# A fused attention and gated MLP kernel on one core: the written order of its operations is made anew from chunk 0's first product to chunk 7

## The chip, the core and the metric

The kernel runs on one core of a Trainium2 chip. That core has five engines with a queue each: TensorE (PE, with its weight loads shown as PEld), VectorE (DVE), ScalarE (ACT), GpSimd (POOL) and SyncE (SP). Each engine works through its own queue strictly in order, and waits at an instruction until the semaphores that it names have come. DMAs are issued from SyncE's, GpSimd's and ScalarE's queues. The metric is the device time of one execution in microseconds.

## What is computed

The reference is a linear attention followed by a two-layer MLP with a SiLU.

```python
# q, k, v: (8 batches, 8 heads, 576 positions, 64); w_in: 512x2048; w_out: 2048x512
q_s = softmax(q, axis=-1)                      # over the 64 of a head
k_s = softmax(k, axis=2)                       # over the 576 positions
kv  = einsum('bhsd,bhse->bhde', k_s, v)        # one 64x64 matrix per head
x   = einsum('bhsd,bhde->bhse', q_s, kv)       # then heads side by side: 4608 x 512
h   = x @ w_in
out = (h * sigmoid(h)) @ w_out                 # 4608 x 512
```

## The kernel before

The 4608 rows of x are cut into nine **chunks** (0 to 8) of 512 rows, while attention works by **batch** (0 to 7) of 576 rows. Chunk 0 is treated as wide: its first product takes all 576 rows of batch 0, and the 64 rows too many are handed to chunk 1 (`gcopy`).

Nearly all the work is written as small named operations, which the text ORDER (lines 18 to 66) lists in one sequence; line 807 calls them one after the other. There is no other scheduler: the place of a name in ORDER is its place in its engine's queue. Ahead of line 807 stands a prelude, written out as plain code (lines 545 to 621): the loads of batch 0 on SyncE, warm-up products (`heat`), batch 0's softmax and attention, the loads of w_in (W1) and of the first part of w_out (W2a) on POOL, and the first half of the contraction for the blocks 0 and 2 of chunk 0.

The names, with b a batch, t a chunk, and a number of a head pair, block or part behind them:

- `lq`, `lk`, `lv` load q, k, v (load, line 146). Batches 1 and 2 come through POOL's queue, later ones through SyncE's. `W2b1` to `W2d` load the rest of w_out (load_w2, line 569), `W1a0` to `W1d` stand for the parts of w_in (load_w1, line 563); both change the type on the way and go through POOL. Each name of batch b takes one of two buffers, so a load waits until the operation that reads the earlier contents is done.
- `eq`, `ek` are the exponentials (ACT, lines 163 and 168), `z` the sums of q (DVE, line 207), `n` the normalising (mostly POOL, line 216), `vc` the cast of v (POOL for batches 2 and later, line 144; ACT and DVE for batch 1). `qp1a` and `qp1b` are two adding steps of batch 1's sum on POOL (lines 181, 188). `tr1` and `tc1` transpose batch 1's q on TensorE and copy it out; `tq` does this by a DMA of SyncE for later batches.
- `kv` makes the head matrices (line 248), `kc` normalises and copies them (DVE, lines 259 and 261), `X`/`xt` make x transposed (line 282), and `x...a`/`x...v` copy it from PSUM on ACT or DVE (lines 142, 144).
- Chunk 0: `w` is a block of 128 columns of the first product (wide_mm, line 307), `h` its tanh (ACT, line 320), `v` the rest of the SiLU (DVE, line 323), `p0` to `p15` the second product (line 445), `po` its copy out (lines 458, 460), `os` its stores.
- Chunks 1 to 8: both products are done as 2x2 blocks in seven block products instead of eight, with sums of blocks made beforehand. `WS`, `xs`, `S`, `T` are those sums (DVE, lines 373, 383, 477, 487). `g t.g.i` is block product i of the first product (line 425, TensorE). Between them the running sum in PSUM is copied to a tile h (`s`, on ACT line 142 or DVE line 144), added again (`a`, DVE line 403), and passed through SiLU (`u`, ACT line 409). `b t.i.m` are the block products of the second product (line 503), `sa`, `sb`, `sc` snapshots (ACT, line 519), `wa`, `wb`, `wc`, `wl` the joining of results, `o` the stores. Half of chunk 1's first product is done plainly (`m`, line 335, SiLU `mu`, line 345).

A product that starts a new sum in a PSUM bank has to wait until the copy of the old sum has ended: so `g4.0.6` waits for `s4.0.0a`, `kv2` for `a1.1.1`, `m0` for `u1.1.4`.

The block that the change cuts in two is

```python
def wide_mm(fb, cs):
    for n in range(2):
        for c in cs:
            nc.tensor.matmul(out=PS[:, WIDE[fb] + n, 0:S // 2],
                lhsT=W1[:, c, fb * 128:(fb + 1) * 128],
                rhs=XTS[0][:, c, n * (S // 2):(n + 1) * (S // 2)],
                start=(c == 0), stop=(c == NC - 1))
```

with 16 blocks fb, and NC = 4 parts c of the contraction. W1a0 brings the parts 0 and 1 of blocks 0 to 3, W1a1 the parts 2 and 3.

Of the kernel before, what the change touches and what calls it, by code (L numbers as in the profile page):

```python
# [15 lines left out]


ORDER = """
    lk1.0 w1 lk1.1 w2 h1 w0 h2 v1 w3 h0 W2b1 w5 v0 v2 h3 w4 WS0.1 h5 w6 v3 h4 W2b2 v4 w7 v5 w8 h7 h6 v7 w9
    lv1.0 h8 v6 w11 v8 h9 lv1.1 w10 eq1.0.0 v9 h11 WS0.2 w12 eq1.1.0 v11 h10 w13 WS1.1 eq1.0.1 v10 h12 w15  # L20
    qp1a h13 v12 w14 eq1.1.1 v13 qp1b WS1.2 W2c1 p0 h14 z1.0 ek1.0 p1 z1.1.0 n1.0 z1.1.1 p2 h15 ek1.1 v15 p3
    WS1.4 W2c2 tr1.0 v14 lq2.0 p4 tc1.0a tc1.0b lq2.1 n1.1 p5 W2d p6 lk2.0 T1 vc1.0 lk2.1 p7 tr1.1 lv2.0
    vc1.1a vc1.1b gcopy WS1.3 kv1 lv2.1 tc1.1b p8 tc1.1a kc1 WS0.3 xt1.0 xt1.1 x1.0a x1.1v p9 x1.2a x1.3v
    g1.1.1 xs1.1 xs1.2 xs1.4 g1.1.2 s1.1.0a WS0.4 p10 xs1.3 eq2.0 a1.1.0 p11 eq2.1 z2.0 g1.1.6 g1.1.5
    s1.1.1a z2.1 n2.0 p12 ek2.0 g1.1.7 p13 s1.1.2v n2.1 ek2.1 p14 a1.1.2 g1.1.4 p15 tq2 u1.1.4 g1.1.3 po2v
    vc2.1 po1a m0 po3v po0a a1.1.1 u1.1.0 vc2.0 m1 lk3.0 mu0 m2 T2 lq3.0 mu1 lq3.1 m3 u1.1.2 lk3.1 T3 m4
    lv3.0 u1.1.1 lv3.1 m5 T4 mu2 os0 mu4 kv2 mu5 m6 mu3 kc2 X2.0 mu6 X2.1 x2.0v m7 x2.1a x2.3a x2.2v g2.1.1
    mu7 xs2.1 xs2.2 g2.1.2 s2.1.0v b1.1.0 ek3.0 S1.1 g2.1.6 eq3.1 lk4.0 S1.2 b1.2.0 os1 s2.1.1a b1.1.1 xs2.3
    xs2.4 eq3.0 a2.1.0 g2.1.7 vc3.0 sa1 b1.2.1 lq4.0 z3.1 s2.1.2a g2.1.5 vc3.1 ek3.1 b1.6.0 a2.1.2 n3.1
    lk4.1 g2.1.4 z3.0 g2.1.3 u2.1.0 g2.0.2 u2.1.4 wa1 n3.0 b1.6.1 a2.1.1 u2.1.2 g2.0.1 sb1 S1.3 kv3 tq3  # L30
    s2.0.0a b1.5.0 kc3 u2.1.1 S1.4 g2.0.6 b1.7.0 s2.0.1v lv4.0 ek4.1 b1.7.1 lv4.1 a2.0.0 os3 g2.0.7 sc1
    ek4.0 b1.5.1 s2.0.2v g2.0.5 eq4.0 lk5.0 wc1 lq4.1 g2.0.4 a2.0.2 os2 b1.4.0 vc4.0 lk5.1 z4.0 u2.0.4
    g2.0.3 u2.0.2 b1.3.0 lv5.0 vc4.1 a2.0.1 u2.0.0 lq5.0 b1.4.1 n4.0 X3.0 wl1v X3.1 kv4 x3.0a x3.1v x3.2a
    b1.3.1 kc4 x3.3a xs3.1 u2.0.1 g3.1.1 xs3.2 wb1 g3.1.2 s3.1.0a xs3.3 xs3.4 g3.0.2 S2.1 g3.1.6 S2.2 eq4.1
    b2.2.0 s3.1.1a b2.1.0 z4.1 ek5.0 b2.1.1 a3.1.0 g3.1.7 n4.1 sa2 ek5.1 b2.6.0 s3.1.2v g3.1.5 vc5.0 tq4
    g3.1.4 a3.1.2 u3.1.0 b2.6.1 u3.1.4 S2.3 g3.1.3 sb2 lq5.1 g3.0.1 u3.1.2 a3.1.1 lv5.1 lk6.0 b2.7.0 s3.0.0a
    o1.0 S2.4 b2.2.1 u3.1.1 a3.0.0 g3.0.6 lv6.0 b2.7.1 s3.0.1v eq5.0 g3.0.5 wa2 g3.0.7 sc2 lq6.0 z5.0 b2.4.0
    s3.0.2a lk6.1 b2.5.0 vc5.1 eq5.1 a3.0.2 g3.0.4 o1.1 n5.0 z5.1 g3.0.3 u3.0.4 b2.5.1 a3.0.1 n5.1 u3.0.0
    b2.4.1 wc2 u3.0.2 X4.0 X4.1 kv5 x4.1v x4.0a tq5 wl2v b2.3.0 u3.0.1 x4.3v g4.1.1 xs4.1 x4.2a b2.3.1 xs4.2
    s4.1.0a S3.1 g4.1.2 wb2 g4.1.6 lq6.1 a4.1.0 ek6.1 b3.1.0 xs4.3 s4.1.1a b3.1.1 xs4.4 S3.2 ek6.0 g4.1.5  # L40
    g4.1.7 sa3 eq6.0 b3.2.0 s4.1.2v eq6.1 b3.2.1 lq7.0 kc5 lk7.0 b3.6.0 a4.1.2 lv6.1 lq7.1 g4.1.4 o2.0 wa3
    g4.1.3 z6.0 u4.1.4 b3.5.0 u4.1.0 S3.3 g4.0.1 lk7.1 b3.6.1 a4.1.1 s4.0.0a g4.0.2 sb3 u4.1.1 g4.0.6 a4.0.0
    b3.5.1 s4.0.1a S3.4 b3.7.0 vc6.1 u4.1.2 g4.0.7 z6.1 vc6.0 g4.0.5 s4.0.2a b3.7.1 a4.0.2 n6.1 g4.0.4 sc3
    u4.0.2 g4.0.3 wc3 n6.0 b3.3.0 u4.0.4 a4.0.1 b3.4.0 u4.0.0 X5.0 X5.1 kv6 x5.0a x5.1v tq6 x5.3a x5.2v
    b3.3.1 u4.0.1 xs5.1 g5.1.1 xs5.2 wb3 b3.4.1 s5.1.0v o2.1 ek7.1 g5.1.2 kc6 g5.1.6 wl3a xs5.3 xs5.4 a5.1.0
    lv7.0 b4.2.0 s5.1.1a lv7.1 b4.1.0 S4.1 eq7.1 g5.1.7 ek7.0 b4.2.1 s5.1.2v o3.1 g5.1.5 S4.2 b4.1.1 u5.1.0
    a5.1.2 g5.1.4 sa4 g5.0.2 o3.0 u5.1.4 wa4 g5.1.3 S4.3 u5.1.2 vc7.1 g5.0.1 b4.6.0 a5.1.1 vc7.0 s5.0.0a
    b4.6.1 a5.0.0 u5.1.1 g5.0.6 S4.4 b4.5.0 s5.0.1a b4.5.1 sb4 u5.0.0 g5.0.7 g5.0.5 s5.0.2v b4.7.0 eq7.0
    a5.0.2 b4.7.1 z7.1 g5.0.4 sc4 g5.0.3 b4.4.0 a5.0.1 u5.0.4 b4.4.1 wc4 u5.0.1 X6.0 X6.1 kv7 x6.0v u5.0.2
    x6.3v b4.3.0 x6.1a kc7 b4.3.1 x6.2a xs6.1 xs6.2 g6.1.1 xs6.4 wl4v g6.1.2 S5.1 s6.1.0a b5.1.0 a6.1.0  # L50
    g6.1.6 xs6.3 g6.0.2 wb4 s6.1.1a S5.2 b5.1.1 o4.0 b5.2.0 S5.3 g6.1.7 S5.4 b5.2.1 s6.1.2a z7.0 g6.1.5 sa5
    g6.1.4 wa5 n7.0 b5.6.0 a6.1.2 u6.1.4 b5.6.1 g6.0.1 n7.1 sb5 u6.1.0 g6.1.3 s6.0.0a b5.7.0 a6.1.1 tq7
    b5.7.1 a6.0.0 u6.1.1 g6.0.6 sc5 b5.5.0 s6.0.1a o4.1 g6.0.5 u6.1.2 g6.0.7 b5.5.1 s6.0.2v b5.4.0 wc5
    g6.0.4 a6.0.2 b5.4.1 u6.0.4 b5.3.0 u6.0.2 X7.0 X7.1 x7.0a x7.1v g6.0.3 x7.2a xs7.1 u6.0.0 g7.1.1 x7.3v
    a6.0.1 b5.3.1 s7.1.0a xs7.2 g7.1.2 wl5a u6.0.1 g7.1.6 o5.1 a7.1.0 b6.1.0 s7.1.1a xs7.4 xs7.3 g7.1.5 wb5
    g7.1.7 S6.1 o5.0 b6.1.1 s7.1.2a S6.2 g7.0.2 sa6 a7.1.2 u7.1.0 g7.1.4 S6.3 b6.2.0 u7.1.4 g7.1.3 u7.1.2
    g7.0.1 a7.1.1 b6.2.1 s7.0.0a b6.6.0 wa6 u7.1.1 S6.4 g7.0.6 b6.6.1 s7.0.1v b6.5.0 sb6 a7.0.0 g7.0.7
    b6.7.0 s7.0.2a b6.7.1 b6.5.1 sc6 u7.0.0 g7.0.4 wc6 g7.0.5 u7.0.4 b6.4.0 a7.0.2 b6.3.0 X8.0 X8.1 x8.0v
    g7.0.3 x8.2a x8.1v u7.0.2 b6.4.1 xs8.1 a7.0.1 x8.3a g8.1.1 xs8.3 g8.1.2 s8.1.0a xs8.2 b6.3.1 wl6a u7.0.1
    g8.1.6 wb6 b7.1.0 S7.1 o6.0 s8.1.1a b7.2.0 a8.1.0 g8.1.7 o6.1 xs8.4 b7.1.1 S7.2 s8.1.2a g8.1.5 sa7  # L60
    u8.1.0 b7.2.1 a8.1.2 g8.1.4 S7.3 g8.1.3 u8.1.4 g8.0.2 a8.1.1 u8.1.2 g8.0.1 u8.1.1 b7.6.0 s8.0.0v b7.6.1
    wa7 g8.0.6 a8.0.0 sb7 b7.5.0 s8.0.1a S7.4 b7.7.0 g8.0.7 g8.0.5 s8.0.2v b7.7.1 a8.0.2 b7.5.1 sc7 u8.0.0
    g8.0.4 wc7 g8.0.3 u8.0.4 b7.4.0 a8.0.1 u8.0.2 b7.3.0 u8.0.1 b7.3.1 e1.0 wb7 S8.1b e1.1 o7.0 S8.1a b7.4.1
# [7 lines left out]
def kernel(  # L71
# [474 lines left out]
    nc.vector.memset(warm, 0.0)  # L546
# [2 lines left out]
    for name, src in (("qt", q), ("kt", k)):
        load(0, name, src, 0, nc.sync)  # L550
        if name == "qt":
            load(0, name, src, 1, nc.sync)
    load(0, "vt", v, 0, nc.sync)
    load(0, "kt", k, 1, nc.sync)
    load(0, "vt", v, 1, nc.sync)
# [19 lines left out]
    heat(20)  # L575
    exp_q(0, 0)
    qsum(0, 0)
    exp_q(0, 1)
    nc.gpsimd.tensor_copy(gate, st[0]["kt", 0][0:1, 1, 0:1])
    load_w1(0, 4, 0, 2)  # L580
    load_w1(0, 4, 2, 4)
    load_w1(4, 8)
    load_w1(8, 12)
    load_w1(12, 16)
    load(1, "qt", q, 0, nc.gpsimd)
    load(1, "qt", q, 1, nc.gpsimd)
    load_w2(0, 4)

    qnorm(0, 0, nc.vector)
    qsum(0, 1)  # L590
    exp_k(0, 0)
    tr(0, 0, 0, 5, 0)
    tr(0, 0, 5, J, 1)
    heat(7)
    qnorm(0, 1, nc.vector)
    vcast(0, 0, nc.scalar)
    trcopy(0, 0, 0, 5, 0, nc.scalar)
    trcopy(0, 0, 5, J, 1)
    kv(0, 0)
    kvcopy(0, 0, 1)  # L600
    tr(0, 1, 0, 5, 2)
    tr(0, 1, 5, J, 3)
    exp_k(0, 1)
    xt_mm(0, 0, 0, 320, 4, 0)
    xt_mm(0, 0, 320, 256, 0, 0)
    heat(3, 6)
    vcast(0, 1, nc.scalar, 0, 1)
    vcast(0, 1, nc.vector, 1, 2)
    trcopy(0, 1, 0, 5, 2, nc.scalar)
    trcopy(0, 1, 5, J, 3)  # L610
    kv(0, 1)
    kvcopy(0, 1, 2)
    heat(2, 3)
    xt_evac(0, 0, 4, 0, 320, 0, nc.scalar)
    xt_evac(0, 0, 0, 0, 256, 320, nc.vector)
    xt_mm(0, 1, 0, 320, 6, 0)
    xt_mm(0, 1, 320, 256, 2, 0)
    wide_mm(0, (0, 1))
    xt_evac(0, 1, 6, 0, 320, 0, nc.scalar)
    xt_evac(0, 1, 2, 0, 256, 320, nc.vector)  # L620
    wide_mm(2, (0, 1))
# [217 lines left out]
```

## Time and profile before

| what | value |
|---|---|
| median of 3 runs | 257.08 us (256.99 to 257.14) |
| profiled execution | 258.61 us, span of its instructions 256.6 us |
| TensorE busy | 249.1 us, 97% of the span |
| DVE, ACT, POOL busy | 206.2, 190.9, 65.8 us |
| DMA, mean over the span | 179 GB/s |
| chunk 0's first product begins | 14.96 us after the span's start |
| chunk 1's first `g2.1.1` | 61.69 us |
| last product ends | 248.6 us |

The profile is of one execution. Times in it count from the first instruction; "busy" is the time in which an engine works on an instruction, and the idle time before an instruction is put down to what ended it. Products overlap one another: a product of 256 columns takes 0.27 us from start to end, but the next starts 0.109 us later, so a group of eight takes 0.87 us from start to start. Times below that compare groups go from start to start.

### The profile page before, as it was taken

What the parts mean: (1) busy time and instruction counts of PE and PEld (TensorE: products, weight loads), DVE (VectorE), ACT (ScalarE), POOL (GpSimd) and SP (SyncE); (2) the same over time, 40 slices, a digit from 0 to 9 for tenths busy, and PEclk for the clock granted to TensorE, in tenths of its full rate; (3) what the DMA queues carried; (4) which work ended last, traced back from release to release, by engine and by line L of the source; (5) the groups of instructions that cost most, each with busy time, mean ns of one, the idle gap of its engine ahead of it and who ended that gap; (6) DMA issues with size and microseconds to landing.
All of it is one profiled execution on the core that took longest, in us unless ns stands there. A gap on an engine that the chain in (4) does not pass through costs nothing.

```text
span 256.6 us, 6459 instructions
## 1 busy us (share of the span) xinstructions
PE 249.1 (97%) x2732; PEld 204.2 (80%) x2732; DVE 206.2 (80%) x276; ACT 190.9 (74%) x225; POOL 65.8 (26%) x62
## 2 busy tenths in 40 slices
PE   8799999999999999999999999999999999999994
...
GB/s 248 348 181 297 302 301 283 351 140 393 378 128 213 403 187 137 361 335 168 276 266 68 224 236 3 3 52 32 163 14 153 13 0 4 148 18 0 66 141 123
DMA packets 36044, 45.89 MB, mean 179 GB/s; under 512 B 16288, under 2 KB 21088, under 8 KB 36016
## 3 DMA queue, kind: packets, MB, share of 16 engines
...
## 4 chain that ended last, share of the span: by engine, by line
PE 76%; DMA 11%; issue 5%; POOL 3%; ACT 2%; DVE 1%; ACTq 0%; POOLq 0%
PE PS L503 37%; PE PS L425 33%; DMA qt<-in_q_dram 5%; DMA kt<-in_k_dram 5%; PE PS L335 3%; PE PS L248 2%; PE PS L282 2%; POOL W L564 1%; DMA out_dram<-ow 1%; POOL qt L152 1%; DVE GT L323 1%; ACT L409 0%; POOL W L570 0%; ACT sg L320 0%; ACT GT L409 0%
## 5 line engine op out<-in xcount | busy, mean ns | idle before, releaser
L403 DVE TENSOR_TENSOR h<-PS,h 128x1024 f32<-128x1024 f32 (+1 forms) x45 | 54.2, 1206 | 9.3 <-PE PS L425 7.8
L503 PEld LDWEIGHTS <-GT 128*128 128x128 f16 x512 | 50.1, 98 | 5.9
L425 PEld LDWEIGHTS <-WS 128*128 128x128 f16 x480 | 46.7, 98 | 6.5 <-issue 0.6
L409 ACT ACTIVATE GT<-h 128x1024 f16<-128x1024 f32 (+1 forms) x45 | 46.8, 1051 | 0.9 <-DVE h L403 0.7
L503 PE MATMUL PS<-W,GT 128*128 128x256 f16 x384 | 47.3, 273 | 0.0
L425 PE MATMUL PS<-XS,WS 128*128 128x256 f16 (+1 forms) x360 | 45.0, 272 | 0.0
L142 ACT COPY h<-PS 128x1024 f32<-128x1024 f32 (+1 forms) x31 | 31.1, 1003 | 16.9 <-PE PS L425 15.7
L503 PEld LDWEIGHTS <-S 128*128 128x128 f16 x384 | 37.1, 98 | 4.6
L425 PEld LDWEIGHTS <-W 128*128 128x128 f16 x360 | 35.2, 98 | 4.4
L216 POOL TENSOR_TENSOR eq<-eq,rzq 128x1152 bf16<-128x1152 bf16 x13 | 27.3, 2115 | 37.6 <-DVE rzq L211 36.3
L503 PE MATMUL PS<-T,S 128*128 128x256 f16 x256 | 32.2, 273 | 0.0
L144 POOL CAST vaug<-vt 128x1152 bf16<-128x1152 f32 x12 | 15.8, 1328 | 61.5 <-DMA vt<-in_v_dram 61.4
L425 PE MATMUL PS<-XT,W 128*128 128x256 f16 (+1 forms) x240 | 29.7, 272 | 0.0
L144 DVE COPY h<-PS 128x1024 f32<-128x1024 f32 (+1 forms) x14 | 17.0, 1212 | 9.2 <-PE PS L425 4.4
L207 DVE TENSOR_REDUCE zq<-eq 128x18 f32<-128x1152 bf16 x14 | 18.8, 1342 | 4.1 <-ACT eq L163 4.0
L163 ACT ACTIVATE eq<-qt 128x1152 bf16<-128x1152 f32 (+1 forms) x18 | 18.9, 1055 | 3.1 <-DMA qt<-in_q_dram 2.8
L168 ACT ACTIVATE ek<-kt 128x1152 bf16<-128x1152 f32 x16 | 18.6, 1163 | 3.0 <-DMA kt<-in_k_dram 2.9
L791 POOL DMA_DIRECT2D out_dram<-ow x5 | 2.7, 545 | 70.0 <-DVE ow L773 70.0
L409 ACT ACTIVATE GT<-PS 128x1024 f16<-128x1024 f32 (+1 forms) x15 | 15.2, 1013 | 6.1 <-PE PS L425 6.1
L503 PE MATMUL PS<-T,GT 128*128 128x256 f16 x128 | 16.3, 272 | 0.0
L307 PE MATMUL PS<-XT,W 128*128 128x288 f16 x128 | 16.0, 286 | 0.2 <-DMA W<-in_moe_w_in_dram 0.2
L503 PE MATMUL PS<-W,S 128*128 128x256 f16 x128 | 16.1, 273 | 0.0
...
## 6 DMA issues: line engine op xcount, KB each, us to landing
...
```

The source lines that it names most:

```text
L142: eng.copy(out=o, in_=i)
L144: eng.tensor_copy(o, i)
L163: nc.scalar.activation(out=half(st[b]["eq"], cc)[:, :, g0:g1], in_=jgd(b, "qt", cc)[:, :, g0:g1], func=ACT.Exp)
L168: nc.scalar.activation(out=half(ek, cc), in_=jgd(b, "kt", cc), func=ACT.Exp)
L207: nc.vector.reduce_sum(out=z, in_=e, axis=AX.X)
L216: eng.tensor_tensor(out=e, in0=e, in1=r[:, :, :, None].to_broadcast([128, J, 2, D]), op=ALU.mult)
L307: nc.tensor.matmul(out=PS[:, WIDE[fb] + n, 0:S // 2], lhsT=W1[:, c, fb * 128:(fb + 1) * 128], rhs=XTS[0][:, c, n * (S // 2):(n + 1) * (S / ...
L335: nc.tensor.matmul(out=PS[:, bank, o0:TCH], lhsT=W1[:, c, fb * 128:(fb + 1) * 128], rhs=XTS[t % 2][:, c, o0:TCH], start=(c == 0), stop=(c ...
L403: nc.vector.tensor_tensor(out=four(t, i), in0=group_bank(t, g), in1=four(t, i), op=ALU.add)
L409: nc.scalar.activation(out=group_out(t, f, n), in_=x, func=ACT.Silu, scale=1.0 / XS)
L425: nc.tensor.matmul(out=PS[:, bank + p // 2, (p % 2) * HT:(p % 2) * HT + width(t)], lhsT=a[:, c, p * 128:(p + 1) * 128], rhs=bb[:, c, 0:wid ...
L503: nc.tensor.matmul(out=PS[:, bank, m * HN:(m + 1) * HN], lhsT=a[:, fc, m * 128:(m + 1) * 128], rhs=bb[:, fc, :], start=(first and fc == 0) ...
```

## The change

The prelude from the loads of batch 0 on becomes named operations too (`lq0.0`, `heat0`, `eq0.0`, `W1a0` and so on), with the same contents, and stands at the head of ORDER. Chunk 0's blocks become two operations each:

```diff
     for fb in range(NFB):
-        op(f"w{fb}", wide_mm, fb, range(2 if fb in (0, 2) else 0, NC))
+        op(f"w{fb}.0", wide_mm, fb, (0, 1))
+        op(f"w{fb}.1", wide_mm, fb, (2, 3))
```

ORDER is then written anew up to chunk 7; from `g8.1.4` on it is the old one. The prelude's operations keep their order on each engine, up to `x0.1`. SyncE's transfers keep theirs. Everything else is reordered, and no operation is added or dropped; the numbers of instructions on each engine stay. The places that matter below, old (-) and new (+), other names left out:

```diff
 first product, chunk 0
-    w1 w2 w0 w3 w5 w4 w6 w7 w8 w9 w11 w10 w12 w13 w15 w14 p0
+    w1.0 w1.1 w0.1 w2.1 w3.0 w3.1 w5.0 w4.0 w4.1 w5.1 w6.0 w7.0 w6.1 w7.1 w9.0 w8.0 w8.1 w9.1 w11.0 ... p0
 POOL, after W2a
-    lk1.0 lk1.1 W2b1 W2b2 lv1.0 lv1.1 qp1a qp1b W2c1 n1.0 W2c2 lq2.0 lq2.1 W2d lk2.0 lk2.1 lv2.0 lv2.1 n2.0 n2.1
+    W2b2 W2b1 lv1.0 lk1.1 qp1a lk1.0 lv1.1 qp1b W2c1 W2c2 n1.0 lq2.0 lq2.1 W2d lk2.0 lk2.1 lv2.0 n2.0 lv2.1 n2.1
 TensorE, chunk 1
-    p10 p11 g1.1.6 g1.1.5 p12 g1.1.7 p13 p14 g1.1.4 p15 g1.1.3 m0 m1 m2 m3 m4 m5 kv2 m6 X2.0 X2.1 m7 g2.1.1 g2.1.2
+    p10 g1.1.6 p11 p12 g1.1.7 g1.1.5 p13 g1.1.4 p14 g1.1.3 p15 m0 m1 m2 m4 m5 m3 kv2 m6 X2.0 X2.1 m7 g2.1.1 b1.1.0
 DVE, from a1.1.2 on
-    po2v po3v a1.1.1 T2 T3 T4 kc2 x2.0v x2.2v xs2.1 xs2.2 s2.1.0v S1.1 S1.2 xs2.3 xs2.4 a2.1.0 z3.1 a2.1.2 z3.0 wa1
-    a2.1.1 S1.3 kc3 S1.4 s2.0.1v a2.0.0 s2.0.2v wc1
+    T1 T2 T3 WS0.3 a1.1.1 WS0.4 po3v kc2 po2v x2.0v xs2.1 x2.2v xs2.2 s2.1.0v S1.1 xs2.4 xs2.3 a2.1.0 S1.2 z3.0 a2.1.2
+    z3.1 a2.1.1 wa1 S1.3 S1.4 a2.0.0 s2.0.1v T4 s2.0.2v kc3 wc1
 ACT, batch 1
-    h14 ek1.0 h15 ek1.1 tc1.0a vc1.0 vc1.1a gcopy tc1.1a x1.0a
+    h15 vc1.0 h14 ek1.1 ek1.0 tc1.0a vc1.1a tc1.1a gcopy x1.0a
 ACT, chunk 1
-    u1.1.4 po1a po0a u1.1.0 mu0 mu1 u1.1.2 u1.1.1 mu2 mu4 mu5 mu3 mu6 x2.1a
+    u1.1.4 po0a u1.1.2 mu0 mu1 u1.1.0 po1a mu2 mu5 mu4 u1.1.1 mu3 mu6 x2.1a
 TensorE, chunk 4
-    g4.0.1 b3.6.1 g4.0.2 g4.0.6
+    g4.0.1 X5.1 b3.5.1 g4.0.6
```

More of the change, by code (lines that the diff above doesn't have):

```diff
@@ L18 @@
 ORDER = """
[L19 to L63, printed above, removed]
@@ L64 @@
-    S8.2a sa8 S8.2b e2.0 wl7v e6.0 S8.3 o7.1 e6.1 e2.1 sb8 e5.0 waE0 S8.4 qa00g qa01s e7.0 waE1 e7.1 qa11g
-    qa10a e5.1 sc8 wcE0 e3.0 wcE1 qc01g wxE0 qc11a e3.1 wbE0 qc00a wxE1 qb00g qb01s e4.0 wbE1 qc10s qb10g
+    lq0.0 lq0.1 lk0.0 lv0.0 lk0.1 lv0.1 heat0 eq0.0 z0.0 eq0.1 gate W1a0 W1a1 W1b W1c W1d lq1.0 lq1.1 W2a n0.0 z0.1
+    ek0.0 tr0.0 heat1 n0.1 vc0.0 tc0.0a tc0.0b kv0.0 kc0.0 tr0.1 ek0.1 X0.0 heat2 vc0.1a vc0.1b tc0.1a tc0.1b kv0.1
+    kc0.1 heat3 x0.0a x0.0v X0.1 w0.0 x0.1v x0.1a w2.0 w1.0 w1.1 w0.1 h1 w2.1 v1 h0 w3.0 v0 h2 w3.1 w5.0 W2b2 w4.0
@@ new lines @@
+    h3 v2 w4.1 w5.1 v3 h4 w6.0 h5 v4 W2b1 w7.0 w6.1 v5 lv1.0 WS1.1 WS0.1 w7.1 h7 w9.0 w8.0 h6 v7 w8.1 v6 h8 w9.1 h9
+    lk1.1 eq1.0.1 eq1.0.0 w11.0 v8 w11.1 h11 v9 qp1a w10.0 lk1.0 w10.1 lv1.1 w12.0 h10 qp1b v11 w13.0 v10 eq1.1.1
+    w12.1 w13.1 w15.0 h12 h13 eq1.1.0 v12 W2c1 v13 w14.0 z1.0 w14.1 w15.1 p0 WS1.2 W2c2 h15 v15 z1.1.0 WS1.4 p1
+    vc1.0 n1.0 lq2.0 z1.1.1 h14 ek1.1 p2 p3 n1.1 ek1.0 p4 tr1.0 p5 tc1.0a v14 tc1.0b p6 tr1.1 WS1.3 vc1.1a tc1.1a p7
+    vc1.1b tc1.1b kv1 kc1 p8 xt1.0 xt1.1 gcopy WS0.2 x1.0a x1.2a x1.1v x1.3v lq2.1 p9 W2d lk2.0 xs1.1 xs1.2 lk2.1
```

117 lines of the change are left out of this document (64 added, 53 removed).

## Prediction

> **What bounds the kernel now.** I read the busy shares, the chain of work that ended last, TensorE's waits, and the timelines of the engines. The page gives
>
> ```profile
> PE 249.1 (97%) x2732; PEld 204.2 (80%) x2732; DVE 206.2 (80%) x276; ACT 190.9 (74%) x225; POOL 65.8 (26%) x62
> PE   8799999999999999999999999999999999999994
> PE 76%; DMA 11%; issue 5%; POOL 3%; ACT 2%; DVE 1%; ACTq 0%; POOLq 0%
> ```
>
> TensorE (PE) is the bound, and the order can only take away its waits. TensorE's waits, over the whole span, are few:
>
> ```profile
> PE PS L234 <- DVE eq L216: 1.3, 2, 0.9
> PE PS L561 <- DVE XS L546: 1.2, 1, 1.2
> PE PS L335 <- ACT GT L409: 0.6, 1, 0.6
> PE PS L445 <- DMA W<-in_moe_w_out_dram: 0.3, 1, 0.3
> PE PS L307 <- DMA W<-in_moe_w_in_dram: 0.2, 1, 0.2
> ```
>
> The first two lie before chunk 0's first product. All others end at 54.13 us; asked from 61 us to 250 us, the same view is empty. Products follow each other there at 0.87 us for 8, and that is the pace that the change can at best keep. So the prize is in the first 54 us, and the risk in everything after it.
>
> What ends those waits is seen in TensorE's timeline
>
> ```profile
> 16.55 14.63 PE L307 MATMUL PS<-XT,W 128*128 128x288 f16 x118 [0.19 <-DMA W<-in_moe_w_in_dram]
> ...
> 47.62 1.02 PE L445 MATMUL PS<-W,GT 128*128 128x512 f16 x4 [0.30 <-DMA W<-in_moe_w_out_dram]
> ```
>
> and in the chain, whose last DMA before 54 us is a load of k:
>
> ```profile
> 38.30 12.31 DMA kt<-in_k_dram
> ...
> 51.87 1.28 ACT L409
> 53.16 0.93 ACT GT L409
> ```
>
> Two landings gate the start: W2d at 47.6 us releases p12, and lk2.1 at 50.61 releases ek2.1, the table load and u1.1.4, which ends at 54.08 and releases m0 at 54.13. In windows from 8 to 51 us the DMA's busy share is 1.00 to 1.21 throughout, so both landings are set by bytes.
>
> **The change, part by part.** A time below is a start or duration of the profiled execution; two queued operations of DVE or ACT overlap by some 0.1 us, so I take start to start.
>
> 1. Halves of w1 and w0.1 ahead of w2.1. w1's third matmul needs W1a1, and the row above shows 0.19 us of idle there. In halves, four matmuls stand ahead of that need, not two: 2 x 0.12 = 0.25 us of cover. All of it (and 0.28 us that TensorE loses before tr1.0, by start to start) is worth nothing at the end if p12 still waits for W2d.
>
> 2. POOL's queue. W2b, lv1.0 and lk1.1 go first, lk1.0 and lv1.1 come behind qp1a, and lv2.1 behind n2.0. The transfers ahead of W2d and of lk2.1 are the same set as before, on one queue that stays filled (lk1.0's issue moves from 14.62 to about 28.3 us, behind qp1a's 1.28 us, while four transfers still wait), so I leave both landings where they are. lk1.0 then lands at about 36.5 us and not 31; ek1.0 follows, and kv1 still starts at about 39 us. TensorE reaches p12 at about 46.2 us, 1.4 us early. Gain at p12: none, the wait is only longer.
>
> 3. p12 to m0. One group, g1.1.5, moves behind p12. Before: 0.86 + 0.77 + 2x0.86 + 0.77 + 0.86 + 0.77 = 5.75 us from 47.62, and 0.76 us lost for u1.1.4. Now: 5.75 + 0.77 = 6.52 us, and m0 at 54.14. g1.1.5 fills what was a wait for u1.1.4, and the wait for W2d grows by as much. Net 0.0.
>
> 4. 54 to 62 us. T1, WS0.3, WS0.4 move here from 37 to 44 us, T4 leaves. On DVE from a1.1.2's end at 51.73: T1, T2, T3 at 1.14 each, WS0.3, WS0.4, po3v at 0.61 each, a1.1.1 at 1.0, 6.25 us, to 58.0; kc2 has to wait for kv2 until 59.75. The 1.8 us of cover holds the port waits below (at most 2 x 1.1). po2v comes before x2.0v: 60.45 + 0.6 = 61.0 against 60.89, and m7's end at 61.69 hides it. ACT does the same set from 53.16 in another order; mu6 waits for m6 as now. 0 to 0.4 us; I take 0.
>
> 5. DVE from 62 to 80 us. This is where I expect the loss.
>
> ```profile
> 62.95 1.22 DVE L144 COPY h<-PS 128x1024 f32<-128x1024 f32 x1
> ...
> 74.23 1.75 DVE L477 TENSOR_TENSOR GT<-GT 128x2048 f16<-128x2048 f16 x1
> 75.91 0.18 DVE L259 RECIPROCAL rz<-PS 128x4 f32<-128x4 f32 x1
> 76.12 0.49 DVE L261 TENSOR_TENSOR kvn<-PS,rz 128x128 bf16<-128x128 f32 x2
> 76.53 1.22 DVE L477 TENSOR_TENSOR S<-GT,S 128x2048 f16<-128x2048 f16 x1
> 77.69 1.22 DVE L144 COPY h<-PS 128x1024 f32<-128x1024 f32 x1
> 78.83 1.21 DVE L403 TENSOR_TENSOR h<-PS,h 128x1024 f32<-128x1024 f32 x1
> ```
>
> Without a gap worth naming, DVE works from s2.1.0v (62.95) to s2.0.1v (77.69), which ends at 78.91; g2.0.7 starts on TensorE at 79.16. The cover is 0.25 us. Now xs2.1 stands ahead of x2.2v and has to wait for x2.0v, so s2.1.0v starts about 0.25 us later. Behind it, up to s2.0.1v, kc3 leaves (76.53 - 75.91 = 0.62) and a2.0.0 comes in (1.14). s2.0.1v starts at 77.69 + 0.25 + 1.14 - 0.62 = 78.46 and ends at 79.68; g2.0.7 would be 0.52 us late. T4 comes right behind s2.0.1v, where DVE waited for g2.0.7 anyway, and costs nothing.
>
> 6. Collisions with POOL. T2 (1.65 us at 54.79) and T3 (2.17 us at 56.36) run beside POOL's two casts (54.20 to 57.46), T4 of the same shape takes 1.21 us at 58.45 with POOL idle; S1.3's 1.75 us beside n3.0 stands against 1.22 us for the other S. So a DVE operation with both inputs in SBUF can lose 0.4 to 1.0 us beside POOL. S1.2 moves from 65.34 to about 67.3 us, where POOL casts v of batch 3 (66.89, 2.63 us for two): 0 to 1.1 us, and S1.3 may lose its 0.53 us. I take +0.2 for both, by the S1.3 row. The Trainium skill, "SBUF — State Buffer", section "Who interferes with whom", says that a VectorE instruction with two SBUF inputs and a GpSimd instruction that reads SBUF exclude each other, whichever issued first holding the ports for its whole length. The trace agrees: T2 ends 1.2 us after the first cast's end, T3 1.1 us after the second's. By that rule S1.2 would wait for the rest of a cast, 0.7 us, and the sum would be 0.5 us higher.
>
> 7. Chunk 4's g4.0.1. It is followed by X5.1 and b3.5.1 alone before g4.0.6, which reuses the bank that s4.0.0a copies. Now that copy starts 0.25 us after the product's end (126.82 against 126.57) and takes 1.01; with 0.04 for the return 1.30 us. X5.1 is half of a 0.46 us pair, b3.5.1 0.87: 1.10 us of cover. Late by 0.2 us; before, b3.6.1 and g4.0.2 (1.74 us) hid it.
>
> 8. Chunks 5 to 7. Counted in the same way, every other such return that the old order does not have too keeps 0.04 us of cover or more: 0, with 0.2 us as the upper end for many thin covers. SyncE's order is the same.
>
> Sum: 0 + 0 + 0 + 0.52 + 0.2 + 0.2 = 0.92 us. The profiled execution has 256.6 us of span in 258.61 us; it becomes about 259.5. The median of the three runs stands 1.53 us below that execution, at 257.08; so I forecast **258.0 us**, 0.4% slower. Ends: without 5's late arrival and the collisions +0.2; with S1.2 at its worst (0.9 more), 4's 0.4 and 8's 0.2, +2.2.
>
> **Rivals.**
>
> *No change within 0.2%* (256.57 to 257.59; about what a measurement of this kernel can tell from no change). s2.0.1v comes in time, because S1.3 no longer meets n3.0 (-0.53) and S1.2 meets no cast. Then only the bank of g4.0.6 is left: 257.08 + 0.2 = 257.3 us. For it: the casts come when v has landed, and tq2 goes out about 1 us earlier. Against: DVE's 0.25 us of cover. Chance 0.26.
>
> *Faster: the landings come earlier.* W2d and lk2.1 are slowed in a patch: from 42 to 44 us the DMA moves 173 and 205 GB/s, from 45 to 49 us 379 to 408. If a new order of the queue takes that patch away, W2d lands up to 1 us earlier, u1.1.4 with it, and TensorE, which now has work in front of m0, uses it: 257.08 - 1.2 + 0.4 = 256.3 us. Against: same bytes, same queue, same neighbours of W2d. That the halves and the shorter waits ahead of p12 alone gain (0.25 + 0.28) needs the same early landing. Chance 0.14.
>
> *Slower by more: k of batch 1 late.* POOL holds lk1.0 until qp1a has run, and ACT does ek1.1, ek1.0, tc1.0a, vc1.1a in one row behind it. If lk1.0 lands after 37.9 us (36.5 by my count, plus the 1.4 us of cover at p12), each further us shifts p12, and with it the end. At 39 us: 258.0 + 1.1 = 259.1 us. Chance 0.10.
>
> That the change doesn't do what it says can be left out: SyncE's rows are the same, and the other queues carry the new order.
>
> **How the numbers follow.** Forecast (258.0) 0.50, no change (257.3) 0.26, early landings (256.3) 0.14, late k (259.1) 0.10. The range of 8 in 10 leaves out half of the early landings and half of the late k: 256.6 to 259.1. Faster by over 0.2%: 0.14. Slower by over 0.2%: the forecast and late k, 0.60. Within: 0.26.
>
> **What would show it.** Step 2 and 3: TensorE's row of p12 starts at 47.6 with about 1.4 us of wait, m0 at 54.1 with none. Step 5: a new wait of g2.0.7 (L425) for DVE's h (L144) of about 0.5 us near 79.5 us. Step 6: S1.2 longer than 1.22 us. Step 7: a wait of L425 for ACT's h (L142) of 0.2 us near 130 us. I am wrong if p12 starts before 47 us, if TensorE has no wait from 61 us on, or if waits show in chunks 5 to 7.

## The result, and the profile after

The changed kernel takes 260.14 us (median of 4 runs, 259.74 to 261.45) against 257.11 us (4 runs, 256.99 to 257.73) measured beside it: a ratio of 1.0122, 95% interval 1.0081 to 1.0162. Measured again (e9 below) the ratio was 1.0113 (1.0095 to 1.0130). So the changed kernel is 3.0 us slower; 0.92 us slower was forecast. The profiled execution took 259.84 us, with a span of 257.9 us.

On its page TensorE is still the bound; it works 1.2 us longer than before, and DVE 3.1 us longer, though neither has an instruction more:

```profile
PE 250.3 (97%) x2732; PEld 204.6 (79%) x2732; DVE 209.3 (81%) x276; ACT 190.5 (74%) x225; POOL 65.9 (26%) x62
...
PE 73%; DVE 11%; DMA 6%; ACT 5%; issue 1%; SPq 1%; POOL 1%; ACTq 0%; POOLq 0%; DVEq 0%
```

TensorE's waits (engine, line, what it waited for: us in total, times, the longest) have changed their releasers. The waits for W2d, W1a1 and the SiLU of L409 are gone, and waits for DVE's copies and additions of h and for a SiLU of DVE (L323) have come. The second to fourth line lie ahead of chunk 0's first product:

```profile
PE PS L425 <- DVE h L144: 1.3, 2, 1.0
PE PS L554 <- DVE XS L546: 1.2, 1, 1.2
PE PS L248 <- ACT vaug L142: 0.7, 2, 0.5
PE PS L234 <- DVE eq L216: 0.2, 1, 0.2
PE PS L248 <- DVE h L403: 0.2, 1, 0.2
PE PS L234 <- DVE GT L323: 0.2, 1, 0.2
```

In TensorE's timeline (start, us, what) chunk 0's first product has no wait, p12 (46.47, within a row of L445) has none, and the waits of L425 and L248 stand at g1.1.4 (50.86) and kv2 (59.05):

```profile
15.31 15.85 PE L307 MATMUL PS<-XT,W 128*128 128x288 f16 x128
...
50.86 0.93 PE L425 MATMUL PS<-XS,W 128*128 128x224 f16 x8 [0.96 <-DVE h L144]
...
54.11 4.70 PE L335 MATMUL PS<-XT,W 128*128 128x448 f16 x24
59.05 0.82 PE L248 MATMUL PS<-vaug,ek 64*64 64x65 bf16 x72 [0.23 <-DVE h L403]
```

DVE's timeline has no gap above 0.11 us from 45.5 to 59.5 us, and three operations with both inputs in SBUF are slow, xs1.4 (46.61), T2 (53.24) and T3 (55.23). The reduction z2.1 (48.22) takes its usual 1.34 us, though POOL rests at that time:

```profile
46.61 1.68 DVE L383 TENSOR_TENSOR XS<-XT,XS 128x448 f16<-128x448 f16 x1
48.22 1.34 DVE L207 TENSOR_REDUCE zq<-eq 128x18 f32<-128x1152 bf16 x1
...
49.77 1.03 DVE L144 COPY h<-PS 128x896 f32<-128x896 f32 x1
...
51.92 1.29 DVE L487 TENSOR_TENSOR T<-W 128x2048 f16<-128x2048 f16 x1
53.24 2.06 DVE L487 TENSOR_TENSOR T<-W,T 128x2048 f16<-128x2048 f16 x1
55.23 2.17 DVE L487 TENSOR_TENSOR W<-W 128x2048 f16<-128x2048 f16 x1
...
57.92 1.07 DVE L403 TENSOR_TENSOR h<-PS,h 128x896 f32<-128x896 f32 x1
```

What runs on POOL in that time is n2.0, n2.1 and the two casts of v:

```profile
45.93 2.11 POOL L216 TENSOR_TENSOR eq<-eq,rzq 128x1152 bf16<-128x1152 bf16 x1 [6.67 <-PE PS L425]
...
50.02 2.11 POOL L216 TENSOR_TENSOR eq<-eq,rzq 128x1152 bf16<-128x1152 bf16 x1 [1.27 <-DVE rzq L211]
52.49 3.83 POOL L144 CAST vaug<-vt 128x1152 bf16<-128x1152 f32 x2 [0.37 <-DMA vt<-in_v_dram]
```

xs1.4 (0.39 us in the old order) starts while n2.0 runs and ends 0.25 us after it. z2.1 stands behind it, then s1.1.2v (49.77), and g1.1.4 needs s1.1.2v's bank: TensorE loses 1.12 us from start to start. a1.1.1 (57.92) ends at 58.99, and kv2 waits for its bank: 0.40 us. The chain that ended last, which in the trace of before came through a load of k, goes through n2.0, the load of v behind it on POOL's queue, and DVE:

```profile
45.93 2.07 POOL eq L216
48.00 3.90 DMA vt<-in_v_dram
...
53.24 2.06 DVE T L487
```

Further on g2.1.6 loses 0.18 us and g2.0.7 0.49 (both wait for a copy of h, L144), and before all these tr1.1 0.38 (for v14, L323). In DVE's timeline WS1.4, which delays v14, takes 1.52 us beside n1.0, S1.2 takes 1.47, and s2.0.1v, which g2.0.7 waits for, starts at 78.93:

```profile
33.34 1.52 DVE L373 TENSOR_TENSOR WS<-W,WS 128x1024 f16<-128x1024 f16 x1
...
67.66 1.47 DVE L477 TENSOR_TENSOR S<-S,GT 128x2048 f16<-128x2048 f16 x1
...
78.93 1.21 DVE L144 COPY h<-PS 128x1024 f32<-128x1024 f32 x1
```

The spans of the two profiled executions differ by 1.3 us only. The one of before, at 258.61 us, was 1.5 us above its own median; e1 shows what that hides.

### The profile page after: what moved, and what is told of

The parts are those of the page before. It is cut to its first block, busy times and chain, and to the rows that moved or that the text cites. A ratio compares the mean times of both kernels' runs of the same rounds, so it can differ in the third digit from the quotient of the medians.

```text
span 257.9 us, 6456 instructions
## 1 busy us (share of the span) xinstructions
PE 250.3 (97%) x2732; PEld 204.6 (79%) x2732; DVE 209.3 (81%) x276; ACT 190.5 (74%) x225; POOL 65.9 (26%) x62
## 4 chain that ended last, share of the span: by engine, by line
PE 73%; DVE 11%; DMA 6%; ACT 5%; issue 1%; SPq 1%; POOL 1%; ACTq 0%; POOLq 0%; DVEq 0%
PE PS L503 33%; PE PS L425 31%; DMA vt<-in_v_dram 5%; PE PS L307 4%; DVE h L403 2%; PE PS L282 2%; PE PS L248 2%; PE PS L445 1%; DVE T L487 1%; ACT eq L163 1%; DVE GT L323 1%; DVE WS L373 1%; SPq L152 1%; DVE h L144 1%; DVE W L487 1%
## 5 line engine op out<-in xcount | busy, mean ns | idle before, releaser
L425 PEld LDWEIGHTS <-WS 128*128 128x128 f16 x480 | 46.7, 98 | 6.7 <-issue 0.9
L409 ACT ACTIVATE GT<-h 128x1024 f16<-128x1024 f32 (+1 forms) x45 | 46.9, 1051 | 0.9 <-DVE h L403 0.8
L425 PE MATMUL PS<-XS,WS 128*128 128x256 f16 (+1 forms) x360 | 44.2, 272 | 0.3 <-DVE h L144 0.3
L425 PEld LDWEIGHTS <-W 128*128 128x128 f16 x360 | 35.1, 98 | 5.6 <-issue 1.4
L144 POOL CAST vaug<-vt 128x1152 bf16<-128x1152 f32 x12 | 16.1, 1348 | 59.8 <-DMA vt<-in_v_dram 48.5
L425 PE MATMUL PS<-XT,W 128*128 128x256 f16 (+1 forms) x240 | 29.4, 272 | 0.0
L144 DVE COPY h<-PS 128x1024 f32<-128x1024 f32 (+1 forms) x14 | 16.9, 1207 | 5.0 <-PE PS L425 4.8
L409 ACT ACTIVATE GT<-PS 128x1024 f16<-128x1024 f32 (+1 forms) x15 | 15.3, 1018 | 7.7 <-PE PS L425 7.6
L425 PE MATMUL PS<-XS,W 128*128 128x256 f16 (+1 forms) x120 | 15.4, 272 | 1.0 <-DVE h L144 1.0
```

What stands on the lines that cost most here:

```text
L144: eng.tensor_copy(o, i)
L409: nc.scalar.activation(out=group_out(t, f, n), in_=x, func=ACT.Silu, scale=1.0 / XS)
L425: nc.tensor.matmul(out=PS[:, bank + p // 2, (p % 2) * HT:(p % 2) * HT + width(t)], lhsT=a[:, c, p * 128:(p + 1) * 128], rhs=bb[:, c, 0:wid ...
```

## The experiments

All times are medians; each ratio is against runs of the kernel before that were measured together with it, whose medians were 257.02 us (e1 to e4), 257.21 (e5 to e8) and 257.42 (e9 to e12). An operation is moved by moving its name in ORDER.

**e1: the new code with the whole old order.**

```diff
-    w0.0 x0.1v x0.1a w2.0 w1.0 w1.1 w0.1 h1 w2.1 v1 h0 w3.0 v0 h2 w3.1 w5.0 W2b2 w4.0
+    w0.0 x0.1a x0.1v w2.0 lk1.0 w1.0 w1.1 lk1.1 w2.1 h1 w0.1 h2 v1 w3.0 w3.1 h0 W2b1 w5.0 w5.1
...
```

> The code of the changed kernel with the whole old order; the blocks of chunk 0 that can run in halves are written as two halves back to back, which is the old sequence of matmuls. It isolates the rewriting from the order, and gives a second trace of the old order. Theory: the profiled execution of the kernel before was not a typical one. Its loads were late (W2d landed at 47.58 us, lk2.1 at 50.61), and its span of 256.6 us is 1.5 us longer than the timed runs allow (257.1 us less the 1.9 to 2.0 us around the span is 255.1 to 255.2). In a typical run W2d lands near 45.6 us as in the changed kernel, the three waits before m0 (0.28 before tr1.0, 0.46 at p12, 0.76 for u1.1.4) are gone, m0 starts near 52.6 us, and the time is 257.1 us (+-0.2%). Rival: the old order itself is late, m0 starts at 54.1 us in every run, and the time of 257.1 us comes from somewhere else; then the trace shows p12 waiting for W2d again.

Measured: 257.12 us, ratio 1.0007 (0.9990 to 1.0023). The trace (257.64 us, span 255.8) has W2d landing at 46.79 us and lk2.1 at 49.81, 0.8 us earlier than the first trace, p12 doesn't wait for W2d, and m0 starts at 53.34 us. Of TensorE's waits behind chunk 0's start one is left:

```profile
PE PS L335 <- ACT GT L409: 0.5, 1, 0.5
```

Rewriting alone costs nothing, and the order is the cause. This wait, in front of m0, hangs on lk2.1's landing. In the traces of e3 and e12, which have the old queue of POOL too, lk2.1 lands at 48.48 and 48.51 us, there is no wait, and m0 starts at 52.55 and 52.41. So a typical run of the old order has m0 near 52.6 us; the first trace, at 54.13, had the latest landings of all 14 profiled executions. e6, whose head is the old order as well, has m0 at 52.63. The expectation that the 0.28 us before tr1.0 go with early landings was wrong: they are in this trace too, and e3, e5 and e6 still lose 0.09 to 0.16 us there.

**e2: new order up to m0, old order from there. e3: old order up to m0, new order from there.**

```diff
 e2, against the new order: from m0 on
-    u1.1.4 p15 po0a T2 m0 u1.1.2 mu0 m1 mu1 u1.1.0 m2 tq2 m4 m5 po1a T3 mu2 WS0.3 m3 a1.1.1
+    u1.1.4 p15 po0a T2 WS0.3 WS0.4 tq2 po2v vc2.1 po1a m0 po3v a1.1.1 u1.1.0 vc2.0 m1 lk3.0
...
 e3, against the old order: from m0 on
-    u1.1.4 g1.1.3 po2v vc2.1 po1a m0 po3v po0a a1.1.1 u1.1.0 vc2.0 m1 lk3.0 mu0 m2 T2
+    u1.1.4 g1.1.3 po2v vc2.1 po1a po0a T2 m0 u1.1.2 mu0 m1 mu1 u1.1.0 m2 m4 m5 T3 mu2 m3 a1.1.1
...
```

> The new order up to m0 (the first product of the mix behind chunk 0, at 54.1 us), the old order for all that is left from there. Theory: about half of the loss is made ahead of m0, because z2.1 and so s1.1.2v come late on DVE and TensorE loses 1.12 us in front of g1.1.4, where a typical run of the old order has no wait; the other half is DVE's order from 54 to 80 us. Then this kernel is 1.1 to 1.5 us slower than before: 258.2 to 258.6 us, with g1.1.4 waiting for s1.1.2v. Rival A (the prediction's steps 3 and 5): all loss is behind m0, and this kernel stands at 257.1 us. Rival B: all loss comes from the head, 260.1 us.

> The old order up to m0, the new order for all that is left from there (T1, WS0.3, WS0.4 and tq2 have then been issued early, as in the old order, so DVE has 2.4 us less between 52 and 58 us). Theory: no wait of kv2 for a1.1.1 (0.40 us), the waits of g2.1.6 (0.18) and g2.0.7 (0.49) stay: 0.7 to 1.0 us slower than before, 257.8 to 258.1 us, with m0 near 52.6 us. Rival A: all loss is behind m0: 260 us. Rival B: all of it is in the head: 257.1 us.

Measured: e2 262.09 us, ratio 1.0193 (1.0172 to 1.0215); e3 258.01 us, 1.0040 (1.0014 to 1.0067). e3 came out as expected in time, with m0 at 52.55 and no wait at kv2; at g2.0.7 it lost 0.29 us and at g2.1.6 0.12, less than the 0.49 and 0.18 expected. e2 missed by 3.5 us. Beside g1.1.4's wait of 1.0 us, that of the changed kernel, its TensorE has

```profile
PE PS L425 <- DVE XS L383: 1.6, 1, 1.6
...
PE PS L248 <- DVE h L403: 0.9, 1, 0.9
```

These are the old order's tail behind the new head: T2, WS0.3 and WS0.4 stand ahead of a1.1.1, T2 (2.06 us at 52.82) and WS0.3 (1.63 us at 54.80) run beside POOL's casts (52.02 to 55.91), kv2 waits for a1.1.1, which starts at 58.16 (the second line), and DVE stays late until S1.2 (2.06 us at 66.90) meets the next casts, and so does xs2.3 (68.88) behind it, for which a product waits (the first line):

```profile
68.88 1.37 DVE L383 TENSOR_TENSOR XS<-XT 128x512 f16<-128x512 f16 x1
```

So head and tail don't add up (5.1 and 1.0 us against 3.0): in e2 a late DVE makes new collisions.

**e4: the changed kernel with xs1.4 earlier.**

```diff
-    xs1.3 g1.1.2 p10 s1.1.0a z2.0 g1.1.6 eq2.1 p11 lv2.0 a1.1.0 xs1.4 p12
+    xs1.3 xs1.4 g1.1.2 p10 s1.1.0a z2.0 g1.1.6 eq2.1 p11 lv2.0 a1.1.0 p12
```

> The changed kernel with one operation of DVE moved: xs1.4 stands right behind xs1.3, where in the changed kernel it stands behind a1.1.0 and runs beside POOL's n2.0 (1.68 us at 46.61 against 0.38 us for the same operation at 43.43 in the old order). Theory: n2.0's hold of the shared SBUF port delays xs1.4, this delays z2.1 and s1.1.2v, and g1.1.4 waits 1.12 us; moved, xs1.4 takes 0.4 us, z2.1 starts near 46 us, the wait in front of g1.1.4 goes, m0 starts near 53.0 us and the time falls by 0.8 to 1.1 us against the changed kernel, to 259.0 to 259.3 us (a part can be given back at kv2, whose wait for a1.1.1 can grow). Rival: z2.1 is late because of its own queue position or n2.0 blocks the next operation in xs1.4's place; then g1.1.4 waits as long as before, and the time stays at 260.1 us.

Measured: 259.21 us, ratio 1.0073 (1.0054 to 1.0091); 0.9 us won, as expected. In DVE's timeline xs1.4 takes 0.39 us, z2.1 starts at 46.76 and takes its usual 1.34 beside n2.0 (46.09 to 48.20), and s1.1.2v comes 1.45 us earlier (chunk 0 began 0.34 us earlier in this execution):

```profile
43.95 0.39 DVE L383 TENSOR_TENSOR XS<-XT,XS 128x448 f16<-128x448 f16 x1
...
48.32 1.03 DVE L144 COPY h<-PS 128x896 f32<-128x896 f32 x1
```

The wait at g1.1.4 is gone; kv2's has grown to 0.73 us.

**e5: xs1.4's new place planted in the old order.**

```diff
-    xs1.2 xs1.4 g1.1.2 s1.1.0a WS0.4 p10 xs1.3 eq2.0 a1.1.0 p11 eq2.1 z2.0 g1.1.6 g1.1.5
+    xs1.2 g1.1.2 s1.1.0a WS0.4 p10 xs1.3 eq2.0 p11 eq2.1 z2.0 a1.1.0 xs1.4 g1.1.6 g1.1.5
```

> The old order with one thing of the new one planted in it: a1.1.0 and xs1.4 stand behind z2.0 on DVE, as in the changed kernel, so that xs1.4 falls beside POOL's n2.0. Theory (the collision with n2.0 is the cause of the late g1.1.4, whatever else the order does): n2.0 runs from about 46.6 to 48.7 us, xs1.4 takes 1.6 to 1.7 us in place of 0.38, z2.1 ends near 50.5, s1.1.2v near 51.5, and g1.1.4, which starts at 50.27 us in the trace of the old order, starts near 51.5: 1.1 to 1.3 us slower than before, 258.1 to 258.3 us, with a wait for DVE's h (L144) in front of g1.1.4. Rival: the old order holds enough cover around g1.1.4 (p13 and p14 stand ahead of it), or xs1.4 is quick there, and the time stays at 257.0 us.

Measured: 258.56 us, ratio 1.0054 (1.0036 to 1.0072). By the ratio it is 1.4 us slower, a little over the 1.1 to 1.3 expected, and not by the expected wait. xs1.4 takes 1.68 us (47.23), but TensorE waits earlier: a1.1.0, moved along, ends at 47.3 us, and g1.1.5 needs its bank.

```profile
47.37 0.93 PE L425 MATMUL PS<-XS,WS 128*128 128x224 f16 x8 [1.47 <-DVE h L403]
```

This wait covers xs1.4's. So e5 shows the collision again, but not its price; that rests on e4.

**e6: e3 with a2.0.0 behind s2.0.1v and xs2.1 behind x2.2v.**

```diff
-    u2.1.1 a2.0.0 tq3 kv3 b1.7.1 s2.0.1v g2.0.7
+    u2.1.1 tq3 kv3 b1.7.1 s2.0.1v a2.0.0 g2.0.7
-    x2.1a lv3.0 xs2.1 x2.3a m7 x2.2v xs2.2
+    x2.1a lv3.0 x2.3a m7 x2.2v xs2.1 xs2.2
```

> e3 (old order up to m0, new order from there) with two operations of DVE moved back: a2.0.0 behind s2.0.1v, and xs2.1 behind x2.2v. Theory (the prediction's step 5): the late s2.0.1v costs 0.29 us in front of g2.0.7 in e3's trace, and the late s2.1.0v 0.12 us in front of g2.1.6; both go, g2.0.7 has no wait, and the time falls by 0.4 us against e3, to 257.6 us. What is left against before (0.6 us) are the thin covers of chunks 2 to 7 and shape switches. Rival: the wait of g2.0.7 is made by the collisions with POOL (S1.2, S1.3) and moves to the next bank (g2.0.5, through a2.0.0); then the time stays at 258.0 us.

Measured: 257.60 us, ratio 1.0026 (1.0007 to 1.0044). s2.0.1v starts 0.87 us earlier than in e3 (75.80 against 76.67), g2.0.7 and g2.1.6 have no wait; kv2 lost 0.30 us in this execution, where T2 took 2.03 us beside a cast. The step of 0.4 us is as expected, but the intervals of e3 and e6 overlap; the traces carry it.

**e7: the old order with p4 ahead of tr1.0. e12: and T1 behind a1.1.2.** Two tries at a kernel faster than both.

```diff
-    p3 WS1.4 W2c2 tr1.0 v14 lq2.0 p4 tc1.0a
+    p3 WS1.4 W2c2 p4 tr1.0 v14 lq2.0 tc1.0a
 e12 also
-    p6 lk2.0 T1 vc1.0 ... a1.1.2 g1.1.4
+    p6 lk2.0 vc1.0 ... a1.1.2 T1 g1.1.4
```

> The old order with p4 moved ahead of tr1.0, as the new order has it, and nothing else. In the old order TensorE loses 0.28 us between p3 and tr1.0, which wait for DVE's n1.0 side; with p4 in that gap this loss goes in the new order's traces. Theory: m0 comes 0.28 us earlier where lk2.1's landing allows it (u1.1.4 can end at 51.95 to 52.1 us with lk2.1 at 48.5, m0 would start at 52.3 to 52.4), and the time falls to 256.7 to 256.8 us: faster than both kernels. Rival: u1.1.4, bound by the landing of lk2.1, ends last in most runs, the gain is lost in front of m0, and the time stays at 257.0 us.

> The old order with p4 ahead of tr1.0 (e7) and T1 behind a1.1.2, where DVE has a gap of 0.85 us. In e7 the 0.28 us gained behind p3 came back as 0.26 us in front of kv1, which waits for tc1.1b, and DVE has no gap from 35.6 us to tc1.1b; T1 is 1.2 us of that stretch. Theory: without T1, tc1.1b is early, kv1 doesn't wait, and TensorE keeps the 0.28 us where lk2.1 lands in time: 256.8 to 256.9 us. Rival A: m0 is bound by u1.1.4, so by the landing of lk2.1, in most runs: 257.0 to 257.2 us. Rival B: T1 beside n2.1 takes 1.7 us and makes a1.1.1 and kc2 late: 257.3 us or more.

Measured: e7 257.36 us, ratio 1.0011 (0.9992 to 1.0030): the 0.28 us are won behind p3, but 0.25 are lost inside kv1, whose second half waits for vc1.1b (it ends at 39.10 us; tc1.1b, which the expectation of e12 names, runs later, at 39.61), and m0 still loses 0.38 us to u1.1.4. e12 257.03 us, ratio 0.9989 (0.9978 to 1.0000): no wait at kv1, m0 at 52.41. That is 0.1% at best, less than these runs can tell from no change. T1 took 1.55 us beside n2.1, where DVE had 0.85 us to spare, and nobody waited.

**e8: e4 with WS1.4 behind v14.**

```diff
-    z1.1.0 WS1.4 p1 ... tc1.0a v14 tc1.0b
+    z1.1.0 p1 ... tc1.0a v14 WS1.4 tc1.0b
```

> e4 (the changed kernel with xs1.4 behind xs1.3) with a second operation of DVE moved away from POOL: WS1.4 behind v14. In the changed kernel and in e4 WS1.4 runs beside POOL's n1.0 and takes 1.52 us, in the old order it stands behind n1.0 and takes 0.73; v14 follows late, and tr1.1, which reuses its bank, waits: TensorE loses 0.38 us behind p6. Theory: WS1.4 takes 0.7 us, v14 ends near 36.4 us in place of 37.7, the 0.38 us go, and the time falls by 0.2 to 0.4 us against e4, to 258.8 to 259.0 us; a part can be given back at kv2, whose wait for a1.1.1 (0.73 us in e4) hangs on DVE's and POOL's work and not on m0. Rival: all of it is given back at kv2, and the time stays at 259.2 us.

Measured: 258.80 us, ratio 1.0055 (1.0035 to 1.0075). WS1.4 takes 0.68 us instead of 1.52, and the loss behind p6 is gone from the trace. The size is as expected, but the interval overlaps e4's. The trace is of a long execution (259.96 us): chunk 0 began at 16.06 us in it, 1.1 us later than in e4's, and S1.2 took 2.04 us beside a cast, which cost 0.63 us at g2.1.3.

**e9: the changed kernel again.** No edit.

> The changed kernel once more, on the chip of the three kernels below, for a tighter ratio and a second trace. Theory: 1.1 to 1.2% slower than before (260.0 to 260.4 us), with the same waits: 1.1 us in front of g1.1.4, 0.4 in front of kv2, 0.5 in front of g2.0.7. Rival: these waits hang on one execution's landings, and come and go; then the second trace shows others.

Measured: 260.45 us, ratio 1.0113 (1.0095 to 1.0130). The second trace has xs1.4 at 1.68 us, T2 at 2.06, T3 at 2.17 and TensorE's losses of 1.03 us at g1.1.4, 0.40 at kv2 and 0.49 at g2.0.7 again, though W2d landed 1.4 us later (46.95). Two more are its own: 0.55 us at p0, behind an exponential that waited for a load of q, and 0.40 at g2.1.3, with S1.2 at 1.82 us.

**e10: e4 with WS0.3 and WS0.4 in earlier gaps of DVE.**

```diff
-    tc1.1b kv1 ... xs1.1 xs1.2 ... mu2 WS0.3 m3 ... vc2.0 WS0.4 kv2
+    tc1.1b WS0.3 kv1 ... xs1.1 WS0.4 xs1.2 ... mu2 m3 ... vc2.0 kv2
```

> e4 (the changed kernel with xs1.4 behind xs1.3), and WS0.3 and WS0.4 moved from DVE's busy stretch at 55 to 59 us into two gaps of DVE ahead of it: WS0.3 behind tc1.1b (gap of 0.49 us at 39.65), WS0.4 behind xs1.1 (gap of 0.52 us at 42.8). Theory (the prediction's step 4, where T1, WS0.3 and WS0.4 were said to cost nothing): WS0.3 alone took 1.63 us there beside POOL's casts, and kv2 waited 0.73 us for a1.1.1; without it a1.1.1 ends in time, the 0.73 us go, the gaps cost 0.1 to 0.2 us, and the time falls by 0.4 to 0.7 us against e4's 259.2 us, to 258.5 to 258.8 us. Rival: the casts hold T1, T2 and T3 all the same and a1.1.1 stays late: 259.2 us.

Measured: 258.38 us, ratio 1.0037 (1.0016 to 1.0058); 0.8 us won against e4, 0.9 by the ratios, a little more than expected. a1.1.1 starts at 54.37 us, and DVE waits for kv2 (2.21 us of idle), not kv2 for DVE. In this execution the casts began only at 54.40 us, behind a late load of v, so T2 and T3 met none; e11 shows the same without that help.

```profile
58.26 0.18 DVE L259 RECIPROCAL rz<-PS 128x4 f32<-128x4 f32 x1 [2.21 <-PE PS L248]
```

What is left in this trace are 0.37 us behind p6 (WS1.4) and 0.74 at g2.0.7, with S1.3 at 2.21 us.

**e11: all of it, in the changed kernel.** The moves of e4, e8, e10 and e6 together.

> The changed kernel with six operations of DVE moved, all else of the new order kept (halves, POOL's queue, TensorE's and ACT's order): xs1.4 behind xs1.3, WS1.4 behind v14, WS0.3 and WS0.4 in the gaps of e10, a2.0.0 behind s2.0.1v, xs2.1 behind x2.2v. Theory: DVE's order, by its collisions with POOL and by two late banks, is the cause of nearly all of the loss. By the single runs: 260.1 - 0.9 (e4) - 0.3 (e8) - 0.6 (e10) - 0.4 (e6) = 257.9 us, 0.2 to 0.4% above before, the rest being shape switches and thin covers. Rival: the mended waits are filled by others (ACT's order, the late v casts of POOL), and the time stays above 258.8 us.

Measured: 257.76 us, ratio 1.0004 (0.9991 to 1.0018): level with the kernel before within these runs' 0.2%. So the places of six operations of DVE account for the loss, as far as these runs can tell; TensorE's, ACT's and POOL's new order stayed. TensorE's waits are the two that lie ahead of chunk 0's first product:

```profile
PE PS L554 <- DVE XS L546: 1.2, 1, 1.2
PE PS L234 <- DVE eq L216: 1.2, 2, 0.9
```

T1 (1.68 us at 50.05) and T3 still meet POOL, but a1.1.1 (55.01) ends at 56.09, 1.0 us before kv2 needs its bank:

```profile
52.91 2.18 DVE L487 TENSOR_TENSOR W<-W 128x2048 f16<-128x2048 f16 x1
55.01 1.08 DVE L403 TENSOR_TENSOR h<-PS,h 128x896 f32<-128x896 f32 x1
```

By ratios the loss goes in these steps: 1.0113 (e9), 1.0073 without xs1.4's collision (e4), 1.0055 without WS1.4's as well (e8) or 1.0037 with WS0.3 and WS0.4 out of the casts' way (e10), 1.0004 with all (e11).

## Why the prediction was right in sign and wrong in size

Point by point, by its steps:

- *The baseline.* This failed first. The sum was made against an execution with three waits that a typical run doesn't have in full: 0.19 us for W1a1 at w1, 0.46 at p12 and 0.76 in front of m0, all behind late landings. No other trace of the old order waits at w1 or p12; in front of m0 e1 and e7 lose 0.68 and 0.38 us, e3 and e12 nothing. Subtracting 1.53 us at the end treats this excess as common to both kernels.
- *1, halves.* Right. From w0.0 to p0 TensorE takes 15.69 us in the changed kernel and 15.69 in e3, which has whole blocks: the halves gain nothing where W1a1 comes in time.
- *2, POOL's queue.* Right for what it moved: lk1.0 landed at 36.34 us (36.5 forecast), kv1 started at 39.39, p12 at 46.47 (46.2 forecast). Wrong that p12 would wait, and so wrong by the prediction's own sign (p12 before 47 us): W2d landed at 45.57. In the seven executions with the old queue W2d lands at 45.5 to 47.6 us, in the seven with the new one at 45.4 to 47.0. The rival "the landings come earlier" had the landings right against the one trace, but they belong to the execution and not to the order, so they bring the change nothing.
- *3, p12 to m0: "Net 0.0", m0 at 54.14.* This step failed, though m0 started at 54.11: that was luck. g1.1.5 was to fill a wait that a typical old run doesn't have, and in its place TensorE waited 1.12 us for s1.1.2v. The step counted TensorE's groups and did not follow DVE to s1.1.2v. Against a typical old run (m0 at 52.6) the step costs 1.5 us and not 0, less up to 0.35 us by which w0.0 began later in this execution. WS1.4's collision at 33 us, which no step looked at, cost 0.38 us of it; p4 ahead of tr1.0 saved 0.09 to 0.28.
- *4, 54 to 62 us: "I take 0".* This failed too. T1 to T3 took 5.40 us from start to start, not 3.42, and a1.1.1 ended at 58.99, not 58.0. The 1.8 us of cover was counted to kc2, but kv2, which waits for a1.1.1, stands ahead of kc2: counted to the end of m3, the last product ahead of kv2 in the new order (six of 0.76 us from 54.11, so 58.66), the cover was 0.7 us. TensorE lost 0.40 us here, 0.73 in e4, and e10 won 0.8 us by clearing it.
- *5, DVE from 62 to 80 us: 0.52.* Right in the path: g2.0.7 lost 0.49 us, by the late s2.0.1v, and e6 took such a wait away. The size is luck in part: in e3 and e4, where S1.2 met no cast (1.22 us), g2.0.7 lost 0.29, so the step's own term was too large and step 6's made up for it. The late s2.1.0v that the step saw cost another 0.18 at g2.1.6, which it didn't see.
- *6, collisions: +0.2 for S1.2 and S1.3.* Right where it looked: S1.2 took 1.47 us, and the 0.20 us by which 0.49 exceeds e3's 0.29 go with it; S1.3 took 1.75 as before. In e9 S1.2 took 1.82 us and cost 0.40 at g2.1.3 besides, nearer to the higher price that the step gave by the rule. But xs1.4 and WS1.4, which no step named, had moved beside POOL as well. The rule from the Trainium skill that the step weighed, "SBUF — State Buffer", section "Who interferes with whom", agrees with the rows: xs1.4 ended 0.25 us after n2.0, S1.3 1.08 us after n3.1 (75.65); T2, which the step has 1.2 us behind the first cast of the old trace, ended 1.1 us behind it. The step applied it to S1.2 alone, where it should have been run over the whole new order.
- *7, chunk 4.* 0.2 forecast; there is no wait at g4.0.6. g4.0.1 and X5.1 take 0.22 us longer together: X5.1 now stands alone among products of another shape, but no run tests that this is the reason. So the number came out by another path than the one forecast.
- *8, the rest 0.* Right: from g3.1.1 on, all other differences of TensorE sum to less than 0.1 us.
- *The sum.* TensorE's losses in the changed kernel's trace add up to 1.12 + 0.38 + 0.40 + 0.18 + 0.49 + 0.22 = 2.79 us, less up to 0.28 for p4: 2.5 us. That trace lies 0.3 us under its median, and e9 loses 0.40 more at g2.1.3. The prediction's upper end was also added up wrong: its terms give +2.4 and not +2.2 us.

What stays open: why W2d and lk2.1 land up to 2.1 us apart from one execution to the next, and whether e12 is really faster. No run moved POOL's operations and left DVE's in place; that POOL is what slows xs1.4, WS1.4 and the others rests on their times with and without POOL at work, and on their ends, which follow POOL's.
